# Biases of two more attention tiles on TensorE, a new opening and a new order in a fused attention and MLP kernel

## Chip, core and metric

The kernel runs on one core of a Trainium2 chip. The metric is the device time of one execution in microseconds; a profile is one profiled execution, and its span runs from the first instruction to the last.

## What is computed

```python
scores = 0.125 * q @ k^T                       # 4 batches, 8 heads, 768 positions, head size 64
keep = (key < 8) | (0 <= query - key < 96)     # 8 global keys, and the 96 last ones
bias = -slope[h] * dist                        # dist = 96 for global keys outside the window
a = softmax(where(keep, scores + bias, -1e9))
x = (a @ v) as rows of 3072 tokens x 512       # all heads of a token side by side
out = relu(x @ w_in) ** 2 @ w_out              # w_in 512 x 2048, w_out 2048 x 512
```

## The kernel before

The 3072 tokens are 24 tiles of 128 (tile j; six to a batch), and 12 blocks of two tiles for the MLP. For each tile: q, k and v are loaded and cast; q and k are transposed (`tr.n.j` on PE, n = 0 for q and 1 for k, and the copy `T.n.j` out of the bank; from tile 8 on by a DMA); `sc` multiplies them into four banks of 128 x 512 scores (head group g, odd or even head; two banks in the first tile of a batch), which hold the tile's own keys and those of the tile before; `exp.j.odd.g` on ACT takes the exponential out of one bank; `pv` multiplies with v, `norm` divides by the sum on DVE, and `trx` with `xT` transposes the result for the MLP. `gk` and `gv` copy the eight global rows of k and v to the tile.

The mask and the bias enter in one of two ways. For tiles under `NBIAS` a matmul ahead of the scores puts them into the bank: `bias.j` multiplies a scaled identity `sid[h]` with the mask `pb`, eight matmuls of 256 columns (of 128 in the first tile of a batch). For the others ACT takes the exponential of the bare scores, and `mul.j.g` on DVE multiplies it by `E`, the exponential of the mask, or by `E0` (made from E) in the first tile of a batch.

The MLP's first layer of blocks 0 and 1 is eight steps `s1.blk.s`, each of one piece of w_in (`win`), with `relu` and `sq`; `s1.0.0` to `s1.0.3` are cut in parts (#1 to #4). From block 2 on it is seven products in place of eight (`h`, with `xs`, `isum`, `u`, `c`, `q` around them); the second layer is `s2`, likewise with `sum`, `wsum`, `part`, `o` and the store `st`.

At the start DVE zeroes a buffer `zero`, and PE multiplies it with itself `NWARM` times (512 columns each). DVE makes `ident32`, `ident`, `pb` and `sid`, and ACT makes E in eight exponentials. Tile 0's q and k come through SP's queue as 32-bit numbers (`plain`); every other load is issued by POOL, which casts to bf16. A second set of `NKEEP` matmuls with `zero`, the operation `warm`, stands behind the transposes of tile 0's q.

The order is written out: a string `ORDER` has one word for each operation, with the bank numbers behind a colon and the engine behind an @; the operations are emitted in that order, so each engine's queue is the order of its words.

```python
nc.scalar.activation(junk, zero[:, :1], Act.Exp)
for i in range(NWARM):
    nc.tensor.matmul(out=banks[7], lhsT=zero[:, :P], rhs=zero, start=True, stop=True)
for g in range(2):
    for odd in range(2):
        for i in range(2):
            nc.scalar.activation(E[:, odd, g, i], pb, Act.Exp, scale=float(slopes[4 * g + 2 * i + odd]))
# per tile
if j < NBIAS:
    bias = plan.op(("bias", j, gs[0]), {"PE": 0.056 * n}, ...)
```

Lines of the profile: 310 and 307 loads, 319 the loads of `plain`, 372 the first warm matmuls, 532 the second, 506 `tr`, 429, 431 and 433 copies by ACT, POOL and DVE, 579 `bias`, 599 `sc`, 665 `exp`, 690 `mul`, 748 `pv`, 778 and 779 `norm`, 816 `trx`, 1061 `s1`, 950 `h`, 1212 and 1339 `s2`, 1287 `o`.

Of the kernel before, what the change touches and what calls it, by code (L numbers as in the profile page):

```python
# [62 lines left out]
T.1.4@V xT.1@V pv.2.1:0 ld.k.5 ld.win.2.0 exp.3.1.1 gk.3@A ld.win.2.1 norm.2.0 s1.0.3:2 mul.3.0 s1.0.6:4 ld.win.4.0
tr.0.4:7 ld.q.5 ld.v.4 norm.2.1 mul.3.1 relu.0.6@A s1.0.3#2 gv.2@P pv.3.0:3 norm.3.0 trx.2:5 T.0.4@A pv.3.1:6
ld.win.1.0 norm.3.1 ld.win.0.1 xT.2@A sc.4.0:1047 exp.4.1.1 exp.4.1.0 tr.1.5:3 T.1.5@A s1.0.2:5 trx.3:6 xT.3@V
ld.win.0.0 ld.win.5.0 s1.0.2#2 s1.0.2#3 s1.0.2#4 relu.0.3@V exp.4.0.1 ld.v.5 gv.3@P exp.4.0.0 gk.4@V sq.0.6@V
relu.0.2@A s1.1.3:7 ld.win.7.0 relu.1.3@A load.6 s1.1.6:0 mul.4.1 tr.0.5:6 mul.4.0 sq.0.3@V s1.1.2:3 T.0.5@A ld.wout.3
pv.4.0:2 ld.wout.1 sq.0.2@V sc.5.0:4157 ld.wout.0 s1.0.4:6 relu.1.2@A exp.5.1.1 s1.0.1:3 sq.1.3@A exp.5.0.0 relu.0.4@V
s1.1.4:7 ld.wout.2 norm.4.0 pv.4.1:4 gv.4@P norm.4.1 sq.0.4@A load.7 exp.5.1.0 sq.1.2@A relu.1.4@A s1.0.0:6 gate.9
ld.wout.4 mul.5.0 s1.0.0#2 sq.1.4@A s1.0.0#3 s1.1.5:2 trx.4:1 exp.5.0.1 relu.1.6@V s1.1.1:4 ld.wout.5 s1.0.1#2  # L70
relu.1.1@A E0.1 mul.5.1 relu.1.5@A pv.5.0:7 s1.1.7:0 s1.1.0:5 sq.1.1@V norm.5.0 ld.wout.6 E0.0 sq.1.5@V tr.1.6:4
sq.1.6@A pv.5.1:2 relu.1.7@A tr.0.6:7 s1.0.0#4 norm.5.1 xT.4@A sq.1.7@A h.2.0.p2:0 ld.wout.7 T.1.6@V h.2.1.p2:1
trx.5:2 xT.5@V relu.1.0@A sq.1.0@A gate.14 h.2.0.p1:5 xs.2.0 s1.0.5:4 sum.1.2 s1.0.7:2 relu.0.1@A xs.2.1 gate.10
sum.1.0 sum.1.1 relu.0.0@A T.0.6@A sc.6.0:36 wsum.0.0 sum.1.3 sq.0.0@A sq.0.1@A s2.0.0.0:7 relu.0.7@A s2.0.1.0 load.9
exp.6.0.0 xs.2.2 s2.0.2.0 exp.6.1.0 s2.0.3.0 s2.0.0.1:2 s2.0.1.1 wsum.2.0 relu.0.5@A sq.0.7@A s2.0.2.1 load.8 mul.6.0
wsum.1.0 s2.0.3.1 tr.0.7:3 tr.1.7:6 gate.15 isum.0.0 h.2.1.p1:4 T.0.7@A s2.0.4.0 isum.0.1 s2.1.p1.0:3 isum.3.1 T.1.7@A
sq.0.5@A pv.6.0:6 isum.1.1 s2.0.4.1 s2.0.5.1 u.2.0.1@A c.2.0.c11 s2.0.5.0 gate.11 u.2.1.1@A h.2.1.p6 q.2.0.c11@A
isum.1.0 T.8 s2.0.6.1 u.2.1.2@A s2.0.6.0 isum.3.0 pv.6.1:0 h.2.0.p6 wsum.2.1 wsum.0.1 s2.1.p1.1 s2.0.7.1 c.2.1.c11
norm.6.0 gate.13 o.0.1@V st.0.1 s2.0.7.0 h.2.1.p7 part.1.p1@A s2.1.p6.0 u.2.0.2@A o.0.0@A u.2.1.3@A h.2.0.p7 h.2.1.p4
T.9 norm.6.1 wsum.3.0 u.2.0.3@A sc.7.0:1762 c.2.1.c21@A wsum.1.1 h.2.1.p5:0 c.2.1.c22 q.2.1.c11@A s2.1.p2.0:4  # L80
exp.7.1.0 exp.7.0.0 isum.2.1 load.10 h.2.0.p4 exp.7.0.1 mul.7.0 exp.7.1.1 s2.1.p2.1 isum.2.0 s2.2.p1.0:7 q.2.1.c21@A
mul.7.1 h.2.0.p5:1 s2.1.p6.1 part.1.p6@A trx.6:6 gate.12 c.2.0.c21@A load.12 pv.7.0:2 xT.6@A c.2.0.c22 q.2.1.c22@A
q.2.0.c22@A s2.2.p1.1 h.2.1.p3 s2.1.p7.0 wsum.3.1 o.1.p2 norm.7.0 h.2.0.p3 pv.7.1:5 s2.1.p7.1 q.2.0.c21@A st.0.0
c.2.1.c12 s2.1.p5.0 s2.1.p5.1 part.1.p7@A q.2.1.c12@A s2.1.p4.0 T.10 s2.1.p4.1 c.2.0.c12 gk.7@V q.2.0.c12@A o.1.p5
o.1.p4@A sc.8.0:6201 st.1.1 part.2.p1@A s2.1.p3.0 norm.7.1 sum.2.0 sum.2.1 s2.1.p3.1 trx.7:5 xT.7@V o.1.p3 h.3.0.p1:3
exp.8.1.0 gk.8@V h.3.1.p1:2 exp.8.0.0 exp.8.1.1 exp.8.0.1 h.3.0.p2:6 xs.3.0 u.3.1.1@A sc.9.0:1540 s2.2.p6.0 mul.8.0
xs.3.1 mul.8.1 u.3.0.1@A h.3.0.p6 exp.9.0.1 exp.9.1.1 gv.7@V h.3.1.p2:4 c.3.0.c11 h.3.1.p6 c.3.1.c11 exp.9.0.0
pv.8.0:0 s2.2.p6.1 pv.8.1:6 load.11 norm.8.0 u.3.1.2@A s2.2.p2.0:1 sum.2.2 gv.8@P q.3.1.c11@A norm.8.1 xT.8 h.3.1.p7
h.3.0.p5:4 u.3.0.2@A h.3.0.p7 s2.2.p2.1 exp.9.1.0 st.1.0 part.2.p6@A xs.3.2 u.3.1.3@A q.3.0.c11@A h.3.1.p5:0 s2.2.p7.0
u.3.0.3@A mul.9.1 mul.9.0 s2.2.p7.1 c.3.1.c22 T.12 c.3.0.c22 pv.9.0:6 h.3.1.p3 o.2.p2 h.3.0.p4 c.3.1.c12 load.15  # L90
norm.9.0 q.3.1.c22@A h.3.0.p3 s2.3.p1.0:5 s2.3.p1.1 c.3.0.c12 q.3.0.c22@A pv.9.1:0 c.3.0.c21@A part.2.p7@A norm.9.1
q.3.1.c12@A h.3.1.p4 q.3.0.c12@A h.4.0.p1:3 c.3.1.c21@A s2.2.p5.0 part.3.p1@A gk.9@V sc.10.0:6402 s2.2.p5.1
q.3.0.c21@A sum.3.0 sum.3.1 s2.2.p4.0 s2.2.p4.1 exp.10.1.0 sum.2.3 exp.10.0.0 exp.10.0.1 h.4.0.p2:4 T.11 u.4.0.1@A
exp.10.1.1 gk.10@V gv.9@A s2.3.p6.0 o.2.p5 mul.10.0 c.4.0.c11 xT.9 h.4.1.p1:6 o.2.p4@A mul.10.1 s2.2.p3.0 s2.2.p3.1
q.3.1.c21@A s2.3.p2.0:0 sum.3.2 u.4.1.1@A pv.10.0:2 pv.10.1:4 s2.3.p6.1 xs.4.0 gate.17 o.2.p3 part.3.p6@A xs.4.1
s2.3.p2.1 norm.10.0 h.4.0.p6 h.4.1.p6 q.4.0.c11@A gv.10@A norm.10.1 u.4.0.2@A load.13 s2.3.p7.0 sc.11.0:7124 u.4.1.2@A
sum.3.3 h.4.0.p7 h.4.1.p7 xs.4.2 exp.11.1.0 o.3.p2 exp.11.0.0 u.4.0.3@V s2.3.p7.1 sc.12.0:17 exp.11.1.1 exp.11.0.1
gate.16 xT.10 h.4.0.p4 c.4.0.c21@A mul.11.0 st.2.0 mul.11.1 h.4.1.p2:4 c.4.1.c11 exp.12.1.0 s2.3.p5.0 pv.11.0:2
pv.11.1:3 s2.3.p5.1 norm.11.0 part.3.p7@A h.4.0.p5:7 q.4.1.c11@A u.4.1.3@A norm.11.1 h.4.1.p5:4 q.4.0.c21@A gate.20
s2.3.p4.0 c.4.0.c22 load.14 s2.3.p4.1 h.4.0.p3 T.13 gate.18 load.16 c.4.1.c22 exp.12.0.0 h.4.1.p4 q.4.1.c22@A h.4.1.p3  # L100
xT.11 s2.4.p2.0:2 h.5.0.p1:3 q.4.0.c22@A o.3.p5 mul.12.0 c.4.0.c12 o.3.p4@A c.4.1.c21@A u.5.0.1@A c.4.1.c12 T.15
s2.3.p3.0 q.4.0.c12@A s2.3.p3.1 q.4.1.c12@V q.4.1.c21@A h.5.0.p2:1 o.3.p3 sc.13.0:5764 st.3.1 st.2.1 h.5.1.p1:0
# [5 lines left out]
c.5.0.c12 q.5.0.c21@A kl.15@V part.4.p7@A c.5.1.c22 q.5.0.c12@A sc.14.0:1346 o.4.p5 s2.4.p4.0 xT.13 exp.14.0.1 kl.14@V
h.5.1.p3 gv.13@P q.5.1.c22@V c.5.1.c12 c.5.1.c21@A s2.4.p4.1 load.17 h.6.0.p1:4 s2.4.p3.0 s2.4.p3.1 exp.14.1.1
exp.14.1.0 exp.14.0.0 sc.15.0:0673 mul.14.1 mul.14.0 xs.6.0 o.4.p4@A xs.6.1 h.6.0.p2:1 o.4.p3 q.5.1.c12@A s2.5.p1.0:5  # L110
u.6.0.1@A c.6.0.c11 exp.15.0.0 exp.15.1.0 exp.15.1.1 sum.5.0 s2.5.p1.1 h.6.0.p6 u.6.0.2@A exp.15.0.1 sum.5.1 load.18
h.6.0.p5:2 part.5.p1@A pv.14.0:0 norm.14.0 pv.14.1:6 h.6.1.p1:1 u.6.1.1@A h.6.0.p7 gv.14@P st.4.0 s2.5.p6.0 u.6.0.3@A
# [96 lines left out]

# [1222 lines left out]
```

## Time and profile before

| | us |
|---|---|
| three runs | 198.62, 199.34, 199.52 |
| median | 199.34 |
| span of the profiled execution | 197.6 |
| PE busy | 191.9 |
| DVE busy | 173.2 |
| ACT busy | 163.0 |
| POOL busy | 80.4 |

The page gives no time of the profiled execution beside its span; the runs were timed apart from it. Busy is the time in which at least one of an engine's instructions ran. Matmuls are pipelined: where many stand in a row, their length by a row of the chain over their number is the pace, while the length of one alone (0.22 us for 128 columns) has the way through the array in it. In a row of the timeline the first number is the start from the span's begin, the second the length, and the brackets tell how long the engine stood idle before and who ended that.

### The profile page before, as it was taken

How to read it: one execution, taken by the hardware profiler on the slowest of the kernel's cores; microseconds unless marked ns; L12 is line 12 of the kernel's file. 1: busy time of each engine (PE TensorE's matmuls, PEld its weight loads, DVE VectorE, ACT ScalarE, POOL GpSimd, SP SyncE). 2: the span in 40 equal slices, each digit the busy share in tenths (PEclk: the TensorE clock that was granted, in tenths of full speed). 3: DMA queues.
4: the chain of work that ended last, by engine and by line, in shares of the span. 5: the costliest groups of instructions: out<-in, count | busy, mean ns of one | idle time of the engine just before them, and what ended most of it. 6: DMA issues, size and time to landing. Idle time of an engine off the chain costs nothing.

```text
span 197.6 us, 6777 instructions
## 1 busy us (share of the span) xinstructions
PE 191.9 (97%) x2776; PEld 169.6 (86%) x2776; DVE 173.2 (88%) x423; ACT 163.0 (82%) x335; POOL 80.4 (41%) x101
## 2 busy tenths in 40 slices
PE   7989999999999999999999999999999999999993
PEld 3578999866989999899989999989899989999992
DVE  8159869999999999799999999999899999989872
ACT  6379989966999898999789998998989879774750
POOL 8999988586045309603192903080410001000000
PEclk9999999999999999999999999999999999999999
DMA  6999999999999999999999999999695711114023
GB/s 127 153 158 171 181 181 185 182 202 159 139 209 191 75 200 88 145 174 210 151 129 203 114 124 194 160 121 92 136 81 116 154 55 56 27 30 163 0 106 106
DMA packets 111857, 26.91 MB, mean 136 GB/s; under 512 B 103379, under 2 KB 109011, under 8 KB 111827
## 3 DMA queue, kind: packets, MB, share of 16 engines
q0 software_dynamic: 80256, 13.37, 91.8%
q1 hardware_dynamic: 31570, 13.11, 32.5%
q8 instruction: 21, 0.34, 0.6%
q14 instruction: 10, 0.07, 0.1%
HBM read 27.26 MB, written 6.29 MB: 170 GB/s over the span
## 4 chain that ended last, share of the span: by engine, by line
PE 95%; DVE 2%; issue 1%; ACT 0%; DVEq 0%
PE bank L1212 35%; PE bank L950 32%; PE bank L1061 7%; PE bank L599 6%; PE bank L748 5%; PE bank L1339 4%; PE bank L372 2%; PE bank L506 2%; PE bank L532 1%; DVE qkT L433 1%; PE bank L816 1%; PE bank L579 0%; ACT qkT L429 0%; DVE o L1287 0%; DVE v L433 0%
## 5 line engine op out<-in xcount | busy, mean ns | idle before, releaser
L1015 ACT ACTIVATE hs<-hr 128x512 bf16<-128x512 f32 x72 | 44.8, 641 | 5.1 <-DVE hr L995 4.7
L665 ACT ACTIVATE esc<-bank 128x512 bf16<-128x512 f32 x78 | 42.9, 614 | 1.3 <-PE bank L599 1.0
L1212 PE MATMUL bank<-wsum,hsum 128*128 128x256 bf16 x264 | 36.2, 273 | 0.0
L1212 PEld LDWEIGHTS <-hsum 128*128 128x128 bf16 x360 | 32.1, 98 | 4.1 <-issue 0.5
L995 DVE CUSTOM_DVE_ANT_0 hr<-bank,early 128x512 f32<-128x512 f32 x45 | 30.4, 685 | 2.5 <-PE bank L950 1.5
L950 PEld LDWEIGHTS <-win 128*128 128x128 bf16 x480 | 29.7, 98 | 1.0
L950 PEld LDWEIGHTS <-qk_first 128*128 128x128 bf16 x480 | 29.7, 98 | 1.0
L429 ACT COPY early<-bank 128x512 f32<-128x512 f32 x42 | 24.5, 591 | 3.6 <-PE bank L950 3.3
L690 DVE TENSOR_TENSOR at<-esc,E 128x1024 bf16<-128x1024 bf16 x39 | 26.7, 696 | 0.1
L1212 PEld LDWEIGHTS <-hs 128*128 128x128 bf16 x264 | 24.0, 98 | 2.6
L310 POOL DMA_DIRECT2D qk<-in_q_dram x18 | 16.0, 890 | 21.9 <-DMA qkT<-qk 20.6
L1212 PE MATMUL bank<-wout,hs 128*128 128x256 bf16 x176 | 24.9, 273 | 0.0
L310 POOL DMA_DIRECT2D v<-in_v_dram x18 | 16.0, 888 | 18.3 <-DVE v L480 14.9
L950 PE MATMUL bank<-xT,win 128*128 128x128 bf16 x320 | 23.4, 219 | 0.0
L431 POOL COPY v<-v 8x520 bf16<-8x520 bf16 x8 | 5.7, 718 | 43.3 <-PE bank L748 43.3
L950 PE MATMUL bank<-xs,qk_first 128*128 128x128 bf16 x320 | 22.8, 219 | 0.0
L779 DVE TENSOR_TENSOR x<-bank,rs 128x256 bf16<-128x256 f32 x48 | 20.4, 425 | 1.7
L865 ACT ACTIVATE hr<-bank 128x512 f32<-128x512 f32 x33 | 19.4, 598 | 1.3 <-PE bank L950 0.4
L748 PE MATMUL bank<-v,at 128*128 128x65 bf16 x352 | 17.8, 193 | 0.0
L1287 DVE TENSOR_TENSOR o<-bank,part 128x256 f32<-128x256 f32 (+2 forms) x34 | 13.8, 410 | 3.3 <-PE bank L1212 3.2
L429 ACT COPY part<-bank 128x256 f32<-128x256 f32 x29 | 10.9, 375 | 7.1 <-PE bank L1212 6.9
L310 POOL DMA_DIRECT2D qk<-in_k_dram x18 | 16.1, 897 | 0.9 <-DMA win<-in_moe_w_in_dram 0.5
(92 smaller groups left out, 367.0 us busy)
## 6 DMA issues: line engine op xcount, KB each, us to landing
out_dram<-o SPq DMA_DIRECT2D x22, 256.0 KB, 2.5
v<-in_v_dram POOLq DMA_DIRECT2D x24, 128.0 KB, 5.6
qk<-in_q_dram POOLq DMA_DIRECT2D x18, 128.0 KB, 5.0
qk<-in_k_dram POOLq DMA_DIRECT2D x18, 128.0 KB, 5.8
wout<-in_moe_w_out_dram POOLq DMA_DIRECT2D x8, 256.0 KB, 8.5
win<-in_moe_w_in_dram POOLq DMA_DIRECT2D x6, 256.0 KB, 6.9
qk_first<-in_k_dram POOLq DMA_DIRECT2D x5, 128.0 KB, 5.6
qk_first<-in_q_dram POOLq DMA_DIRECT2D x5, 128.0 KB, 5.7
```

Source lines behind the costliest of these rows:

```text
L310: nc.gpsimd.dma_start(out=dst, in_=src)
L429: nc.scalar.copy(dst, src)
L665: nc.scalar.activation(out=tiles[tag, j, g][:, odd], in_=tiles.pop(("sc", j, odd, g)).rearrange("p a c -> p (a c)"), func=Act.Exp, scale=s ...
L690: nc.vector.tensor_mul(at, tiles.pop(("esc", j, g)), bias)
L748: nc.tensor.matmul(out=po[:, hi, :], lhsT=tiles["at", j, g][:, odd, at * P : (at + 1) * P], rhs=v_sb[kj][:, h, :], start=(i == 0), stop=(i ...
L779: nc.vector.tensor_tensor(out=x[:, 4 * hf : 4 * hf + 4, :], in0=po[:, :, :D], in1=rs.to_broadcast([P, 4, D]), op=Alu.mult,)
L865: nc.scalar.activation(dst, src, Act.Relu)
L950: nc.tensor.matmul(out=tiles["h", blk, g, bank][:, n], lhsT=left_[:, s, k], rhs=right_[:, k], start=opens and n == 0 and k == 0, stop=k == ...
L995: nc.vector._custom_dve(TENSOR_ADD_SAT, out=hr, in0=src, in1=tiles.pop(("u", blk, g, i)), s0=float("inf"), s1=0.0,)
L1015: nc.scalar.activation(hs, hr, Act.Square)
L1061: nc.tensor.matmul(out=hT[:, c, cols], lhsT=w_in_sb[s][:, kt, c * P : (c + 1) * P], rhs=tiles["xT", blk][:, kt, cols], start=(kt == 0), st ...
L1212: nc.tensor.matmul(out=tiles["acc", blk, bank][:, cols], lhsT=left_[:, s], rhs=right_[:, cols], start=first and s == 0, stop=s == NSTEP - ...
```

## The change

1. `NBIAS` goes from 3 to 5: the bias and mask of tiles 3 and 4 are put into the banks by PE, and their four multiplications on DVE go.
2. `zero` and its memset go; the first warm matmuls use a constant of ones that is written ahead of the program, 16 of 224 columns in place of 8 of 512.
3. The operation `warm` (8 matmuls of 512 columns) goes.
4. The eight exponentials of E become operations `E.odd.g.i` of the order; the multiplications and E0 depend on them.
5. The order is new throughout, the order of the loads and the choice of engines with it: k and q of tile 1 are loaded first, and the piece `win.3.0`, which was first, is ninth.

```diff
-    NBIAS = 3
+    NBIAS = 5
-    zero = early[:, 1, 2 * P :].bitcast(BF16)
-    NWARM = 8
-    NKEEP = 8
+    NWARM, NWCOL = 16, 224
-    nc.vector.memset(zero.bitcast(I32), 0)
+    one = nc.const_aps.tensor(1.0, [P, NWCOL], BF16)
-    nc.scalar.activation(junk, zero[:, :1], Act.Exp)
+    nc.scalar.activation(junk, one[:, :1], Act.Exp)
     for i in range(NWARM):
-        nc.tensor.matmul(out=banks[7], lhsT=zero[:, :P], rhs=zero, start=True, stop=True)
+        nc.tensor.matmul(out=banks[7][:, :NWCOL], lhsT=one[:, :P], rhs=one, start=True, stop=True)
+    maskE = {}
-                nc.scalar.activation(
-                    E[:, odd, g, i], pb, Act.Exp, scale=float(slopes[4 * g + 2 * i + odd])
+                def emit_E(e, g=g, odd=odd, i=i):
+                    nc.scalar.activation(
+                        E[:, odd, g, i], pb, Act.Exp, scale=float(slopes[4 * g + 2 * i + odd])
+                    )
+                maskE[odd, g, i] = plan.op(
+                    ("E", odd, g, i), {"ACT": 0.32}, emit_E, key=-1.0, ready=4.0,
                 )
-            ready=8.0,
+            deps=[m for (o, _, _), m in maskE.items() if o == odd],
-        if j == 0:
-            def emit_warm(e):
-                for _ in range(NKEEP):
-                    nc.tensor.matmul(out=psum(), lhsT=zero[:, :P], rhs=zero, start=True, stop=True)
-            plan.op(("warm",), {"PE": 0.216 * NKEEP}, emit_warm, key=base)
-                deps=exps + (maskE0 if first else []),
+                deps=exps + (maskE0 if first else [m for (_, gg, _), m in maskE.items() if gg == g]),
 ORDER
-tr.0.0:0 warm:7 tr.1.0:1 T.1.0@V bias.0.0:23 T.0.0@A sc.0.0 ld.win.3.0 exp.0.0.0 ld.k.1 tr.1.1:4 bias.1.0:5670 T.1.1@V ld.q.1
+ld.k.1 ld.q.1 E.0.0.1 ld.q.2 E.0.1.0 E.1.1.0 tr.0.0:0 ld.v.0 E.1.0.0 ones.6 T.0.0@A ld.k.2 tr.1.0:1 ld.q.3 bias.0.0:23
```

What it moves is shown at four places. The first is POOL's queue at the start (`qk_first` holds q and k of tiles 1 to 5, `v_0` and `v_1` v of tiles 0 and 1), before:

```order
L367 IOTA early_103 128x256
L307 DMA win_93<-in_moe_w_in_dram 128x4x256
L307 DMA qk_first_66<-in_k_dram 128x8x64
L307 DMA qk_first_66<-in_q_dram 128x8x64
L307 DMA v_0_71<-in_v_dram 128x8x64
L307 DMA qk_first_66<-in_q_dram 128x8x64
L307 DMA qk_first_66<-in_k_dram 128x8x64 x2
```

and after:

```order
L360 IOTA early_103 128x256
L300 DMA qk_first_66<-in_k_dram 128x8x64
L300 DMA qk_first_66<-in_q_dram 128x8x64 x2
L300 DMA v_0_71<-in_v_dram 128x8x64
L300 DMA qk_first_66<-in_k_dram 128x8x64
L300 DMA qk_first_66<-in_q_dram 128x8x64
L300 DMA v_1_72<-in_v_dram 128x8x64
L300 DMA qk_first_66<-in_k_dram 128x8x64
L300 DMA win_93<-in_moe_w_in_dram 128x4x256
```

The piece of w_in went from the first place to the ninth, and tile 1's k and q lead.

The second is PE around the transposes of tile 0's q (bank 0, `bank_107`) and k (bank 1, `bank_108`), before, with the last rows of the second warm set:

```order
L532 LDWEIGHTS early
L532 MATMUL bank_114<-early 128x512
L506 MATMUL bank_108<-ident_100,plain 128x128 x4
L579 LDWEIGHTS early
L579 MATMUL bank_109<-pb_105,early 128x128
```

and after:

```order
L365 LDWEIGHTS const-bfloat16-1.0
L365 MATMUL bank_114<-const-bfloat16-1.0 128x224
L505 MATMUL bank_107<-ident_100,plain 128x128 x4
L505 MATMUL bank_108<-ident_100,plain 128x128 x4
L572 LDWEIGHTS early
L572 MATMUL bank_109<-pb_105,early 128x128
```

Nothing stands between the two transposes any more.

The third is ACT's queue from the masks to the exponentials of tile 2 (the casts and copies into `qkT` are T, the small one of 128x4x8 is gk; the exponentials write `at`), before:

```order
L397 ACTIVATE E_101<-pb_104 128x256 x8
L429 CAST qkT_0_81<-bank_0_107 128x512
L665 ACTIVATE at_198<-bank_2_109 128x512
L665 ACTIVATE at_198<-bank_3_110 128x512
L665 ACTIVATE at_238<-bank_7_114 128x512
L665 ACTIVATE at_238<-bank_0_107 128x512
L665 ACTIVATE at_277<-bank_6_113 128x512
L429 COPY qkT_1_82<-qkT_0_81 128x4x8
L429 COPY qkT_2_83<-bank_1_108 128x512
```

and after:

```order
L392 ACTIVATE E_101<-pb_104 128x256 x4
L428 CAST qkT_0_81<-bank_0_107 128x512
L428 CAST qkT_0_81<-bank_1_108 128x512
L658 ACTIVATE at_212<-bank_3_110 128x512
L392 ACTIVATE E_101<-pb_104 128x256 x2
L658 ACTIVATE at_212<-bank_2_109 128x512
L658 ACTIVATE at_244<-bank_6_113 128x512
L428 COPY qkT_1_82<-qkT_0_81 128x4x8
L428 COPY qkT_2_83<-bank_5_112 128x512
L658 ACTIVATE at_244<-bank_7_114 128x512
```

Four masks stay ahead, two went between the exponentials of tile 0, and k of tile 0 is now cast by ACT (before by DVE).

The fourth is the order's last words. Before, the second piece of the last product, `s2.11.p3.1#2`, came behind the sum `o.11.p3` of the first piece: `s2.11.p3.0 s2.11.p3.1 s2.11.p3.0#2 o.11.p3 s2.11.p3.1#2 st.11.0#2 o.11.p3#2 st.11.0#3`. Now it comes ahead of it: `s2.11.p3.0 o.11.p4 s2.11.p3.1 st.11.1#2 s2.11.p3.0#2 s2.11.p3.1#2 o.11.p3 st.11.0#2 o.11.p3#2 st.11.0#3`.

More of the change, by code (lines that the diff above doesn't have):

```diff
@@ L63 @@
[L63 to L102, printed above, removed]
@@ L108 @@
[L108 to L112, printed above, removed]
@@ L158 @@
[L158 to L160 removed]
+ld.k.1 ld.q.1 E.0.0.1 ld.q.2 E.0.1.0 E.1.1.0 tr.0.0:0 ld.v.0 E.1.0.0 ones.6 T.0.0@A ld.k.2 tr.1.0:1 ld.q.3 bias.0.0:23
+T.1.0@A tr.1.1:4 ld.v.1 sc.0.0 T.1.1 tr.0.1:5 exp.0.1.0 bias.1.0:6701 T.0.1 ld.k.3 E.0.0.0 E.0.1.1 sc.1.0 exp.0.0.0
@@ new lines @@
+ld.win.6.0 pv.3.1:5 norm.3.0 sc.4.0 ld.win.4.0 norm.3.1 s1.0.0:0 exp.4.1.0 s1.0.0#2 gv.3@P trx.2:6 exp.4.0.1 trx.3:4
+xT.2 s1.0.0#3 sq.0.3 s1.0.0#4 ld.win.2.0 xT.3 tr.0.5:5 tr.1.5:2 T.0.5 s1.1.3:7 load.6 T.1.5@A gk.4 relu.0.0 s1.1.0:6
+relu.1.3@V exp.4.0.0 exp.4.1.1 sq.0.0@V sc.5.0:4520 s1.0.5:3 exp.5.1.0 ld.win.2.1 exp.5.1.1 pv.4.0:7 exp.5.0.1 ld.v.5
+s1.0.1:1 norm.4.0 relu.0.5 s1.1.1:5 gate.11 ld.win.7.0 exp.5.0.0 pv.4.1:0 E.1.1.1 mul.5.0 s1.1.6:2 sq.1.3 gv.4@P
+norm.4.1 sq.0.5 s1.0.4:7 load.7 mul.5.1 relu.1.6 s1.0.1#2 sq.1.6@V s1.1.5:3 relu.1.0@V relu.0.4@V trx.4:4 s1.1.4:0
@@ new lines @@
+load.12 h.2.0.p3 c.2.0.c21 s2.0.7.1 wsum.0.1 s2.0.7.0 o.0.1 pv.7.0:3 wsum.2.0 s2.1.p1.1 q.2.1.c22 wsum.1.1 h.2.1.p4
+part.1.p1 pv.7.1:7 norm.7.0 c.2.1.c21 s2.1.p6.0 wsum.2.1 s2.1.p6.1 o.0.0 h.2.1.p3 norm.7.1 part.1.p6 q.2.0.c21
+sc.8.0:5320 st.0.1 c.2.0.c12 h.3.0.p1:7 exp.8.1.0 gv.7 q.2.1.c21@V trx.7:4 exp.8.0.0 s2.1.p7.0 T.10 gk.8 exp.8.0.1
+c.2.1.c12 h.3.0.p2:3 exp.8.1.1 s2.1.p2.0:5 xT.7 s2.1.p2.1 mul.8.0 q.2.1.c12 s2.1.p7.1 u.3.0.1 o.1.p2 sc.9.0:2140 mul.8.1
+q.2.0.c12 s2.1.p5.0 c.3.0.c11 exp.9.0.1 load.11 s2.1.p5.1 exp.9.1.1 gate.13 sum.2.0 pv.8.1:4 part.1.p7 pv.8.0:3 xs.3.0
```

143 lines of the change are left out of this document (86 added, 57 removed).

## The prediction

> **What bounds the kernel now.** I read the page's busy shares and chain first, then stretches of the span, then the opening instruction by instruction, then the landings of the loads, then the end.
>
> ```profile
> PE 191.9 (97%) x2776; PEld 169.6 (86%) x2776; DVE 173.2 (88%) x423; ACT 163.0 (82%) x335; POOL 80.4 (41%) x101
> PE 95%; DVE 2%; issue 1%; ACT 0%; DVEq 0%
> 0.00:17.90 17.90, 15.36 (x173) 10.38 (x174) 9.98 (x45) 11.28 (x26) 17.10 (x25) 1.00 1.79 150
> 17.90:193.90 176.00, 176.00 (x2604) 158.97 (x2601) 162.59 (x378) 151.68 (x311) 63.33 (x77) 1.00 1.21 135
> 10.00 0.87 PE bank L579 x8
> 18.29 1.32 PE bank L1061 x16
> 20.52 0.22 PE bank L816 x4
> 21.11 0.55 PE bank L599 x16
> 161.76 2.18 PE bank L1212 x20
> ```
>
> The first line is the page's busy time, the second its chain by engine, the next two are stretches (PE first, then weight loads, DVE, ACT, POOL), the rest are pieces of the chain (start, us, what). PE is the chain for 95% of the span. From 17.9 us to 193.9 us it is busy in all 176.00 us, and twenty 256-column matmuls in 2.18 us are 0.109 us each, the same 0.109 as the eight of a bias in 0.87 us: matmuls follow each other at one rate, and nothing is waited for. So in that stretch every added column on PE costs its time, and work taken off DVE or ACT brings nothing unless PE waits for it. Time can be gained in the opening 17.9 us and behind 193.9 us only.
>
> ```profile
> 0.74 0.45 SPq L319 DMA_DIRECT2D plain<-in_q_dram  x1
> 0.86 0.27 DVE L361 MEMSET early<- 128x256 int32 x1 [0.86 <-PEq L1413]
> 1.19 3.60 PE L372 MATMUL bank<-early 128*128 128x512 bf16 x8 [1.19 <-DVE early L361]
> 1.25 0.56 SPq L319 DMA_DIRECT2D plain<-in_k_dram  x1
> 1.34 0.89 POOL L307 DMA_DIRECT2D win<-in_moe_w_in_dram  x1 [0.17 <-issue]
> 2.22 0.90 POOL L307 DMA_DIRECT2D qk_first<-in_k_dram  x1
> 3.20 2.56 ACT L397 ACTIVATE E<-pb 128x256 bf16<-128x256 bf16 x8 [0.96 <-DVE pb L386]
> 4.58 1.06 PE L506 MATMUL bank<-ident,plain 128*128 128x128 f32 x4
> 5.43 2.62 PE L532 MATMUL bank<-early 128*128 128x512 bf16 x8
> 7.89 0.60 PE L506 MATMUL bank<-ident,plain 128*128 128x128 f32 x4
> 8.53 0.69 DVE L433 CAST qkT<-bank 128x512 bf16<-128x512 f32 x1 [3.55 <-PE bank L506]
> 9.71 1.09 ACT L665 ACTIVATE at<-bank 128x512 bf16<-128x512 f32 x2 [3.44 <-PE bank L599]
> 12.26 1.57 ACT L665 ACTIVATE at<-bank 128x512 bf16<-128x512 f32 x3 [1.46 <-PE bank L599]
> 13.70 0.23 ACT L429 COPY qkT<-qkT 128x32 bf16<-128x32 bf16 x1
> 13.81 0.61 ACT L429 COPY qkT<-bank 128x512 bf16<-128x512 bf16 x1
> 16.65 0.23 PE L599 MATMUL bank<-qkT 64*128 64x128 bf16 x2 [0.29 <-DVE qkT L433]
> 21.45 0.22 PE L599 MATMUL bank<-qkT,qkT 64*128 64x128 bf16 x2
> plain<-in_q_dram SPq DMA_DIRECT2D x1, 256.0 KB, 3.1
> plain<-in_k_dram SPq DMA_DIRECT2D x1, 256.0 KB, 6.0
> win<-in_moe_w_in_dram POOLq DMA_DIRECT2D x1, 256.0 KB, 5.7
> qk_first<-in_k_dram POOLq DMA_DIRECT2D x1, 128.0 KB, 5.7
> ```
>
> These are rows of the timeline (start, length, engine, line, in brackets the idle time before) and, last, of the DMA view (us from issue to landing, for the first issue of each). PE spends 1.19 to 4.58 on the first warm matmuls and 5.43 to about 7.7 on the second set, both without use for the result. What follows hangs on one instruction: the transposes of tile 0's k at 7.89. They could not have begun before 1.25 + 6.0 = 7.25, when that k landed. Behind them the cast (8.53), the first scores, and the first exponential at 9.71; the scores of tile 3 begin at 16.65, those of tile 4 end at 21.67. I call the start of k's transposes D: D is 7.89, the scores of tile 4 end at D + 13.8.
>
> **The change, part by part.**
>
> *Biases of tiles 3 and 4 on PE.* Sixteen 256-column matmuls at 0.109 us: +1.74. The four multiplications that go from DVE release nothing, since PE waits for DVE nowhere in 17.9 to 193.9. In the new order the bias of tile 3 stands before T.1.3, which ACT gives late (next point), so most of it fills a wait; the bias of tile 4 stands in dense work.
>
> *ACT's order.* Before, all eight mask exponentials (2.56 us, 0.32 each) lay in 3.20 to 5.76, where ACT had nothing else. Now four stand there, two (0.64 us) between the two exponentials of tile 0, one ahead of tile 4's, one later. ACT is serial here. Counted on from D with the rows' pitches (0.52 for one of three exponentials in 1.57, 0.59 for a copy, 0.11 from the small copy to the next): the first exponential starts at D + 1.75 (9.71 less 7.89, and the cast is an ACT copy of some 0.6 in place of 0.69); then one exponential, two masks, two exponentials, the small copy, T.1.2, seven exponentials and T.1.3 are ten times 0.53, 0.64, 0.11 and two times 0.55: 7.2 us, with two hand-overs of 0.1 about D + 9.1. The scores of tile 3 can then begin; before they began at 16.65 = D + 8.76. So they are some 0.4 later behind D, with tile 3's bias done. From there to the end of tile 4's scores stand on PE 0.55 (scores), 0.22, 0.46, 0.89, 0.45, 0.87 (bias of tile 4), 0.46 and 0.55 us, and two waits for DVE (the copy of v's global rows stands behind a relu there) of some 0.3 and 0.1: 4.9, so about D + 14.1 against D + 13.8. But at that point the new order has not done two pieces that the old one had: s1.0.6 (eight 256-column matmuls, 0.87) and trx.2 (0.22). Behind D the new opening is therefore 0.3 + 1.1, about 1.4 to 1.6 us the longer: I take 1.6, as small hand-overs are left out. Were both biases hidden it would be 0; were neither, and the two masks on the chain too, 1.74 + 0.64 = 2.4. The value lies nearest to the walk through the rows.
>
> *Warm matmuls and zeros.* The second set (2.4 us before D) goes; the first set is 16 times 224 columns, at 427 ns per 512 columns (3.60 us for eight, less the fill) 0.19 each, 3.0 us, from a constant that POOL writes ahead of the program, so about 0.4 sooner than behind the memset: it ends near 3.8, beside the landing of q at 0.74 + 3.1 = 3.84. The memset that goes (0.27 us on DVE) was beside other work: 0.
>
> *Loads of tile 1 first.* The 256 KB of w_in that POOL issued first move behind eight others, so each of these lands one issue pitch earlier (0.88, from 1.34 to 2.22): tile 1's k at some 6.4 instead of 7.95. More weight lies on tile 0's k, which goes through SP's queue: 6.0 us against q's 3.1, and it landed at 7.25 just behind w_in's 1.34 + 5.7 = 7.04. I read this as sharing with that transfer. With half the size beside it I put it 0.85 earlier, at 6.4, so D is 6.45. Bounds: no gain, 7.3; as fast as q, 4.4, where PE itself is busy until 4.8: D in 4.8 to 7.3, the gain 0.6 to 3.1. I take 7.89 − 6.45 = 1.44. Seven pitches and its own larger size behind that k, the w_in piece lands at about 13.5, ahead of its first use at some 17; v and the later tiles land as early as before or earlier. SP's queue has the same issues up to there.
>
> ```profile
> PE bank L1212 <- DVE o L1287: 0.5, 1, 0.5
> 193.18 0.94 PE L1212 MATMUL bank<-wout,hsum 128*128 128x192 bf16 x12
> 194.16 0.36 DVE L1287 TENSOR_TENSOR o<-bank,part 128x192 f32<-128x192 f32 x1 [0.84 <-PE bank L1212]
> 194.57 0.28 PE L1212 MATMUL bank<-wout,hsum 128*128 128x64 bf16 x4 [0.45 <-DVE o L1287]
> 194.88 0.22 DVE L1287 TENSOR_TENSOR o<-bank,part 128x64 f32<-128x64 f32 x1 [0.37 <-PE bank L1212]
> ```
>
> *The end* (a row of the waits, four of the timeline). PE's last four matmuls wait 0.5 us for the sum of the first 192 columns. The new order puts them ahead of that sum. They then end 0.5 sooner, but the sum starts 0.1 later and the second follows it directly: the last one ends near 194.85 instead of 195.10, and the two stores still go one behind the other through SP: −0.1, between 0 and −0.3.
>
> *The rest of the order.* About equal numbers of instructions on ACT and DVE, and PE without a wait before. I take 0; the bounds are −0.2 and +0.8, since an order with a new wait can only lose where nothing was lost.
>
> *Sum.* −1.44 + 1.6 − 0.1 = +0.06. The profiled span is 197.6; the median run is 199.34, 1.74 above it, which I take as the time around the span. So 197.66 and 199.4. The three runs spread over 0.9 us, so the profiled one may be up to half a microsecond from the median.
>
> **Rivals.**
>
> *The clock rises later (slower).* Until about 6.8 us PE ran at half speed: the first set took 427 ns per 512 columns (216 by the rate of the long stretch), of the second, eight in 2.62 us, some three did, and k's transposes took 0.60 where q's took 1.06. Before, PE was busy without a gap from 1.19 to 7.7. Now it stands idle from the end of q's transposes (about 4.8) to D. If that delays the rise to some 10 us, the work between D and there (0.60, 0.45, 0.22, 0.40, 0.22 and the bias of tile 1, 0.87: 2.8 us) runs at half speed, and as ACT hides some of it, about 1.3 us is lost, between 0.7 and 2.0: 200.7. It decides from the point at which the clock is still half when D comes. For it: the rise came 5.6 us into gapless work before. Against: the new first set begins earlier and is followed by q's transposes, 3.9 us in one piece.
>
> [...]
>
> *Tile 0's k is not earlier.* If 6.0 us is SP's own time, D is 7.3: the gain is 0.6, and the time 200.2. For it: the transfer was issued as the second of its queue.
>
> *The opening gains all round (faster).* With w_in out of the way k lands by 5.3, D is 5.4, and tile 3's and 4's biases lie in waits (cost 0.8 in place of 1.6): −2.5 + 0.8 − 0.1 = −1.8, or 197.6; half of it is 198.5. Against: ACT's chain holds it then, and v of tile 0 and k of tile 2, which by the pitch land three and four issues behind tile 1's k, near 9 and 9.8.
>
> **How the numbers follow.** The forecast case 0.42 (199.4, own range 198.6 to 200.3), the late clock 0.32 (200.0 to 201.4), k not earlier 0.08, the faster opening 0.18. A difference under 0.5% (1.0 us) cannot be told from none here. Faster than 198.3: two thirds of the last case and little of the first, 0.16. Slower than 200.3: most of the late clock and half of the third case, 0.32. Same: 0.52. The range 198.0 to 201.2 leaves out the ends of the second and the last case.
>
> **What would show it.** The profile after should have k's transposes near 6.5 at 0.60 us; tile 3's scores near 15.6 behind an ACT copy, with PE idle before them; tile 4's scores ending near 20.6; no stretch with idle PE behind 21; 0.5 us less wait at the end. Wrong would be: transposes of 1.06 us at D (the clock), a D of 7.3 or 5.4 (the load), or waits on PE past 21 us (the order).

## The result and the profile after

| | runs | median us | ratio to the kernel before |
|---|---|---|---|
| before, same chip | 198.62 to 199.52 | 199.29 | |
| after | 200.25, 201.02, 201.22, 203.34, 203.43 | 201.22 | 1.0084 (1.0056 to 1.0113) |

The new kernel is 0.8% slower; 1.0084 times the 199.34 us shown before is 201.0. Here and below, a run more than 1.5% above the fastest of its kernel (here the two over 203 us) is left out of the ratio, though not of the median. Its profiled execution was the fastest of the five, 200.25 us with a span of 198.5. The page's busy times and chain, two stretches (PE, weight loads, DVE, ACT, POOL), and the one row that PE's waits between 20 and 194 us have:

```profile
PE 191.9 (97%) x2792; PEld 171.0 (86%) x2792; DVE 175.6 (88%) x424; ACT 159.6 (80%) x328; POOL 80.8 (41%) x102
PE 35%; POOL 1%; DVE 0%; DVEq 0%; issue 0%
0.00:17.90 17.90, 15.88 (x215) 12.67 (x216) 11.52 (x49) 13.96 (x31) 17.08 (x25) 1.00 1.84 151
17.90:193.90 176.00, 175.06 (x2566) 157.53 (x2564) 163.59 (x374) 145.28 (x298) 63.72 (x78) 1.00 1.24 135
PE bank L592 <- DMA qkT<-qk: 0.5, 1, 0.5
```

The stretch in which PE had been busy for all 176.00 us now has 0.94 us of idle PE, 0.65 of it behind 21 us, and a name stands beside PE's longest wait that the old trace did not have: a DMA transpose. The chain's shares sum to little more than a third, so its followed part is of less use here than the stretches. The opening and the end, as rows of the timeline, and the landing of tile 0's k from the DMA view:

```profile
plain<-in_k_dram SPq DMA_DIRECT2D x1, 256.0 KB, 4.0
0.78 3.15 PE L365 MATMUL bank<-const-bfloat16-1.0 128*128 128x224 bf16 x16 [0.78 <-PEq L1406]
4.28 1.66 PE L505 MATMUL bank<-ident,plain 128*128 128x128 f32 x8 [0.35 <-DMA plain<-in_q_dram]
14.60 0.23 PE L592 MATMUL bank<-qkT 64*128 64x128 bf16 x2 [0.48 <-ACT qkT L428]
19.52 0.22 PE L592 MATMUL bank<-qkT,qkT 64*128 64x128 bf16 x2
193.80 1.06 PE L1205 MATMUL bank<-wout,hsum 128*128 128x192 bf16 x16
194.90 0.49 DVE L1280 TENSOR_TENSOR o<-bank,part 128x192 f32<-128x192 f32 x2 [1.22 <-PE bank L1205]
194.40 0.95 SPq L1302 DMA_DIRECT2D out_dram<-o  x1
```

The eight transposes of q and k are one row; the second four begin at 5.27, just behind k's landing (issued 1.26, 4.0 later). So D is 5.27, 2.62 earlier than before, and tile 4's scores end at 19.74.

To place the difference I add to 20 us the matmuls that PE has still to do, each at its pace in the dense stretch. That is when PE would end if it waited for nothing more. It separates opening, middle and end (us, all from one profile each; for a few traces with two or three missing matmul records the work is taken from the complete ones):

| profile | end by the work left at 20 us | PE's last matmul | lost in between | from there to the span's end |
|---|---|---|---|---|
| before | 188.80 | 194.65 | 5.85 | 2.95 |
| after | 188.31 | 194.66 | 6.35 | 3.82 |

Most of the 5 to 6 us lost in between is the change between the score matmuls on 64 rows and all others on 128: from 20 us on the old kernel has some twenty changes each way, of about 0.12 us from 64 rows to 128 and 0.10 back, beyond the pace. PE counts as busy in them, and every version has them. The old end has 0.62 of it in the wait before its last four matmuls, which in the new order lies behind PE's last matmul. So the opening, with both biases paid, is 0.49 ahead; the middle loses 6.35 − (5.85 − 0.62) = 1.12; the end loses 3.82 − (2.95 + 0.62) = 0.25. The sum is +0.88, which is the difference of the spans. The middle is the largest term, and larger still in other executions.

### The profile page after: what moved, and what is told of

Same layout as the page of the kernel before. It is cut to its first block, busy times and chain, and to the rows that moved or that the text cites. A ratio compares the mean times of both kernels' runs of the same rounds, so it can differ in the third digit from the quotient of the medians.

```text
span 198.5 us, 6809 instructions
## 1 busy us (share of the span) xinstructions
PE 191.9 (97%) x2792; PEld 171.0 (86%) x2792; DVE 175.6 (88%) x424; ACT 159.6 (80%) x328; POOL 80.8 (41%) x102
## 2 busy tenths in 40 slices
DMA packets 111857, 26.92 MB, mean 136 GB/s; under 512 B 103378, under 2 KB 109010, under 8 KB 111826
## 5 line engine op out<-in xcount | busy, mean ns | idle before, releaser
L1008 ACT ACTIVATE hs<-hr 128x512 bf16<-128x512 f32 x67 | 41.1, 634 | 5.0 <-DVE hr L988 4.8
L658 ACT ACTIVATE esc<-bank 128x512 bf16<-128x512 f32 x70 | 38.5, 602 | 2.1 <-PE bank L592 1.7
L1205 PE MATMUL bank<-wsum,hsum 128*128 128x256 bf16 x264 | 35.4, 273 | 0.1
L428 ACT COPY early<-bank 128x512 f32<-128x512 f32 x41 | 23.7, 591 | 5.6 <-PE bank L943 4.8
L683 DVE TENSOR_TENSOR at<-esc,E 128x1024 bf16<-128x1024 bf16 x35 | 23.8, 682 | 0.8 <-ACT esc L658 0.5
L943 PE MATMUL bank<-xT,win 128*128 128x128 bf16 x320 | 24.3, 219 | 0.0
L1205 PE MATMUL bank<-wout,hs 128*128 128x256 bf16 x176 | 24.1, 273 | 0.0
L943 PE MATMUL bank<-xs,qk_first 128*128 128x128 bf16 x320 | 23.6, 219 | 0.0
L858 ACT ACTIVATE hr<-bank 128x512 f32<-128x512 f32 x31 | 18.7, 608 | 3.2 <-PE bank L943 2.0
L741 PE MATMUL bank<-v,at 128*128 128x65 bf16 x352 | 17.9, 193 | 0.3 <-DVE v L432 0.3
L741 PEld LDWEIGHTS <-at 128*128 128x128 bf16 x352 | 15.6, 98 | 1.7 <-issue 0.5
```

What stands on the lines that cost most here:

```text
L428: nc.scalar.copy(dst, src)
L658: nc.scalar.activation(out=tiles[tag, j, g][:, odd], in_=tiles.pop(("sc", j, odd, g)).rearrange("p a c -> p (a c)"), func=Act.Exp, scale=s ...
L683: nc.vector.tensor_mul(at, tiles.pop(("esc", j, g)), bias)
L741: nc.tensor.matmul(out=po[:, hi, :], lhsT=tiles["at", j, g][:, odd, at * P : (at + 1) * P], rhs=v_sb[kj][:, h, :], start=(i == 0), stop=(i ...
L858: nc.scalar.activation(dst, src, Act.Relu)
L943: nc.tensor.matmul(out=tiles["h", blk, g, bank][:, n], lhsT=left_[:, s, k], rhs=right_[:, k], start=opens and n == 0 and k == 0, stop=k == ...
```

## The experiments

First four asked which part of the change costs the time: the clock and the idle PE of the opening, the middle's order, the end, or the biases. Runs are given as medians beside the old kernel's median on the same chip.

### The new kernel once more

No edit.

> The changed kernel once more, unaltered, to see what differs between executions. Its first profile (span 198.5) had tile 0's k transposes at 5.3 us and the full clock from 5.0 us, three waits that the old order does not have (sum about 1.1 us past 20 us, the longest 0.5 us for a DMA transpose of tile 11 at 76.9) and an end 0.9 us longer behind PE's last matmul. Theory A (clock): executions differ by when PE's clock rises; a longer one shows transposes of k at 1.06 instead of 0.60 us and the scores of tile 3 at about 16 instead of 14.6. Theory B (loads): the opening is the same, and longer executions wait longer for DMA transposes between 60 and 130 us. Both: median 200.3 to 201.3, that is 1.005 to 1.010 of the kernel before.

201.34 beside 199.57, ratio 1.0091 (1.0050 to 1.0133). Its stretch, and PE's wait rows between 20 and 194 us:

```profile
17.90:193.90 176.00, 174.04 (x2553) 156.67 (x2554) 162.63 (x372) 145.41 (x298) 63.83 (x78) 1.00 1.25 134
PE bank L1205 <- DVE o L1280: 0.7, 1, 0.7
PE bank L592 <- DMA qkT<-qk: 0.7, 2, 0.5
103.67 0.42 DVE L1280 TENSOR_TENSOR o<-bank,part 128x256 f32<-128x256 f32 x1 [0.67 <-DMA out_dram<-o]
```

The opening was the same (188.3 by the work left at 20 us), the clock rose early (4.05 us into the span), and PE's last matmul came 1.17 later than in the first profile. The wait for DVE is one for a transfer too: the last row shows DVE's sum `o` held 0.67 us until an earlier store had left its buffer. The loss is in the middle and differs from execution to execution.

### PE kept busy in the opening

```diff
-    NWARM, NWCOL = 16, 224
+    NWARM, NWCOL, NKEEP = 19, 224, 4
+            plan.op(("warm",), {"PE": 0.1 * NKEEP}, emit_warm, key=base)
 ORDER
- tr.0.0:0
+ tr.0.0:0 warm:7
```

> The changed kernel with PE kept busy until tile 0's k has landed: 19 instead of 16 warm matmuls, and 4 more of them between the transposes of tile 0's q and of k. Theory A (clock): the late rise goes, and the runs come together near the shortest ones of the changed kernel, 200.2 to 200.7. Theory B (loads): the spread stays, and the median is the changed kernel's, or up to 0.4 later as k's transposes begin at about 5.7 instead of 5.3.

203.07 beside 199.57, ratio 1.0176 (1.0138 to 1.0215). The opening stood 0.4 ahead of the new kernel's, and the middle lost 4 us more:

```profile
30.85 0.40 PE L505 MATMUL bank<-ident,qk 128*128 128x128 bf16 x4 [0.20 <-DMA qk<-in_q_dram]
31.52 0.40 PE L505 MATMUL bank<-ident,qk 128*128 128x128 bf16 x4 [0.27 <-DMA qk<-in_k_dram]
55.69 0.23 PE L598 MATMUL bank<-qkT 64*128 64x128 bf16 x2 [0.75 <-DMA qkT<-qk]
```

PE reached tile 6's transposes and tile 8's scores before their transfers had landed. The clock rose at 4.67 us here, early, and the kernel was slower still: a late clock is not the cause.

### The new kernel with the old end

```diff
-s2.11.p3.0#2 s2.11.p3.1#2 o.11.p3 st.11.0#2
+s2.11.p3.0#2 o.11.p3 s2.11.p3.1#2 st.11.0#2
```

> The changed kernel with one word moved back: the last four matmuls (second piece of s2.11.p3.1) behind the sum of the first 192 columns, as before. If the end's 0.9 us come from that word: the sum of 192 columns begins 0.24 us behind the last matmul of the first piece again, the time from it to the last landing is as before, and the kernel is 0.3 to 0.9 us shorter. Rival: the 0.9 us come from SP, whose store ahead of them took 0.95 us to issue in place of 0.40, which the word does not touch: then at most 0.3, and the long issue comes and goes by itself.

201.79 beside 199.57, ratio 1.0115 (1.0085 to 1.0146). From the start of the last sixteen matmuls to the span's end it took 4.5 us (195.40 to 199.9), against 4.7 and 4.4 (193.80 to 198.5, 194.97 to 199.4) in the two profiles of the new end and 4.4 (193.18 to 197.6) before. As far as four profiles tell, the two ends are worth the same; what moves them is how long SP takes to issue one store (`st.11.1#2`), 0.95 in the row above, 0.70 to 0.73 in three others and 0.40 in the old kernel. Why it differs is not shown.

### The old kernel with two more biases

`NBIAS` 5; `bias.3.0` and `bias.4.0` ahead of their scores, the four multiplications out.

> The kernel before with one part of the change: biases of tiles 3 and 4 by PE, each right ahead of its scores, and their four multiplications on DVE left out; all else in the old order. Theory 1 (PE has no idle time past 17.9 us, so each column counts): 16 matmuls of 0.109 us, +1.7 us, less what of tile 3's lies in the wait ahead of its scores (0.45 us): +1.3 to +1.7. Rival (DVE and ACT are the hidden limit in 20 to 50 us, and 2.8 us less on DVE pay for the columns): 0 or shorter.

200.84 beside 199.57, ratio 1.0059 (1.0037 to 1.0080): 1.2 us, of 1.74 on PE. PE waited for nothing between 20 and 194 us. The biases alone cost two thirds of what the whole change costs, and yet they do not explain it: the new opening has already paid for them and is ahead.

### The old order with two parts of the new opening

```diff
-    NKEEP = 8
+    NKEEP = 0
 ORDER
- sc.0.0 ld.win.3.0 exp.0.0.0
+ sc.0.0 exp.0.0.0
- T.1.3@V ld.k.4 pv.1.0:4
+ T.1.3@V ld.k.4 ld.win.3.0 pv.1.0:4
```

> The old order with two things of the new opening alone: the piece win.3.0 goes from the first place of POOL's queue to the ninth, and the second warm set is left out (NKEEP 0); three biased tiles, the zeros and the mask exponentials as before. Theory B (the new order's loss lies behind 20 us, in scores and products set too close behind what they read; the opening itself gains): tile 0's k lands near 5.2, its transposes start near 5.7 instead of 7.89, of the 2.2 us 1.5 to 2.2 are kept, and behind 20 us nothing waits: 197.4 to 198.1, ratio 0.989 to 0.993. Rival R (the middle is held by its loads, whatever the order, and an earlier opening only runs into them): the start is as early, but waits appear between 40 and 100 us and the time is 198.8 to 199.6. Rival C (the second warm set kept the clock): the clock rises behind 8 us, k's transposes take 1.06, 199 to 200.

199.60 beside 199.08, ratio 1.0015 (0.9989 to 1.0040): no gain. Tile 0's k landed at 5.17, D was 5.41, and at 20 us the kernel stood 0.8 ahead of the old one (188.0). Its last matmul came at 194.96, 0.31 behind the old one's. Two rows show where the lead went; the third is the second one's place before:

```profile
33.90 0.40 PE L504 MATMUL bank<-ident,qk 128*128 128x128 bf16 x4 [0.40 <-DMA qk<-in_k_dram]
105.28 0.43 DVE L920 TENSOR_TENSOR xs<-xT 128x512 bf16<-128x512 bf16 x1 [0.82 <-DMA xT<-x]
104.77 0.42 DVE L922 TENSOR_TENSOR xs<-xT 128x512 bf16<-128x512 bf16 x1
```

An earlier PE meets loads and DMA transposes that are not earlier. Before, `xT` took 4.9 us from issue and landed at 104.67, and DVE took it up at 104.77 without a wait, but with 0.1 us to spare; here it was issued 0.4 earlier, took 5.8 and landed at 105.26. For that `xs` PE then waited 0.54 us. The old order's 176.00 busy us had hidden this: it had no wait and, at such places, no reserve.

### The old kernel without its second warm set

`NKEEP` 0, loads as before.

> The old kernel without its second warm set (NKEEP 0), loads unchanged. If the 256 KB of w_in beside tile 0's k set its landing, k lands near 7.25 as before, its transposes start near 7.3, and the time is 0.3 to 0.6 less, 198.8 to 199.1, the clock having risen by then or not. If PE itself (the warm set) was what the start waited for, k lands well before 7 us and the gain is over 1 us, under 198.4. Rival C: PE idle from 5.6 to 7.3 keeps the clock at half until 10 us: 200 to 200.8.

199.51 beside 199.08, ratio 1.0019 (0.9993 to 1.0045).

```profile
4.40 1.35 PE L506 MATMUL bank<-ident,plain 128*128 128x128 f32 x8
8.08 0.40 PE L506 MATMUL bank<-ident,qk_first 128*128 128x128 bf16 x4 [1.14 <-DMA qk_first<-in_k_dram]
106.78 0.34 PE L950 MATMUL bank<-xs,qk_first 128*128 128x128 bf16 x3 [0.86 <-DVE xs L922]
```

k landed at 5.05 with w_in's piece beside it, against 7.25 in the old kernel, 7.74 with five biases and 6.79 in a later run of the same opening (the old order with loads left out, below), and 5.17 to 5.7 in the profiles in which w_in came ninth. So with that piece beside it k landed later in three profiles and as early in one: that the piece held it up is not shown. D was 5.10, and 1.14 us of it went to tile 1's k, at 8.08. Of the 2.8 us that D gained, 0.8 were left at 20 us and none at the end: the early k did not bring the time under 198.4 that was to follow from it.

### The new opening before the old rest

The new kernel's first 116 words, then the old order's words.

> The new kernel with its own first 116 words (up to the copy xT.3, near 22 us) and from there the words of the old order, without the four multiplications of tiles 3 and 4. Theory B: the opening of the new kernel stands about 0.5 us ahead of the old one with both biases paid, and the old rest has no waits: 198.6 to 199.2, ratio 0.995 to 0.999. Rival 'biases': the 1.74 us of the biases are the loss, as in the old order with five biased tiles: 200.3 to 200.8. Rival R (an earlier opening runs into the loads): 199.3 to 200.3 with waits for loads or DMA transposes between 40 and 100 us.

209.19 beside 199.08, ratio 1.0515 (1.0486 to 1.0545). A miss of the experiment itself: the old rest wants another piece of w_in next than the new opening had ordered.

```profile
25.32 1.89 PE L1058 MATMUL bank<-xT,win 128*128 128x256 bf16 x8 [4.71 <-DMA win<-in_moe_w_in_dram]
20.40:25.30 4.90, 0.22 (x4) 0.04 (x1) 0.62 (x2) 0.12 (x1) 4.79 (x6) 1.00 1.62 187
25.30:32.10 6.80, 5.55 (x36) 4.43 (x37) 1.39 (x2) 2.66 (x5) 3.70 (x5) 0.50 1.99 173
```

It cannot tell what the old middle would be worth. It shows that an order of work and an order of loads belong together, and what came behind a long wait of PE: after the 4.71 us the granted clock (the last number but two) is 0.50 for 6.8 us.

### More reserve in the new order

`sc.8.0` behind `s2.1.p7.0`, `sc.9.0` behind `s2.1.p5.1`; `load.11` and `load.12`, `T.11` and `T.12` exchanged.

> The new kernel with its three tight places loosened: the scores of tile 8 stand behind three more pieces of PE's work and those of tile 9 behind two, and the load and DMA transpose of tile 11 go ahead of those of tile 12. Theory B: the waits of 0.4 to 0.6 us of PE for a DMA transpose at 54 and at 77 us go, 0.7 to 1.1 us in all: 200.2 to 200.6 against the new kernel's 201.3, ratio 1.003 to 1.006. Rival: the waits move to another input (the banks, the exponentials behind the later scores) and the time stays at 201.0 to 201.5; or the loss lies in waits elsewhere that differ from run to run, and the time stays as well.

203.17 beside 199.08, ratio 1.0203 (1.0160 to 1.0246): worse by 2 us. The waits for DMA transposes at the three places did go; the reserve (from the transpose's landing to its scores) became 1.3, 2.2 and 4.8 us, from 0.24, 0.48 and 0.05. In their place came:

```profile
56.37 0.33 PE L943 MATMUL bank<-xT,win 128*128 128x128 bf16 x3 [0.47 <-ACT esc L658]
60.68 0.31 PE L741 MATMUL bank<-v,at 128*128 128x65 bf16 x5 [0.68 <-ACT esc L658]
87.69 0.38 PE L1205 MATMUL bank<-wsum,hsum 128*128 128x256 bf16 x2 [1.43 <-ACT part L428]
86.50 0.87 ACT L428 COPY kl<-qkT 128x512 bf16<-128x512 bf16 x2 [1.38 <-DMA qkT<-qk]
```

The later scores make the exponentials late (the first two rows), and the exchange, which sets `load.15` behind `T.12`, made tile 15's DMA transpose late, landing at 86.47 instead of 83.19; for it ACT's copy `kl` stood, and behind it `part`, and PE (the last two).

### Old and new with most loads left out

By now two theories were left for the middle: transfers (R), or hand-overs between PE, ACT and DVE (H). The next three leave out the loads of later tiles. Their output is therefore not the one asked for, and they serve for their time alone.

```diff
             def emit_load(e, j=j):
-                load_v(j)
-                load_part(0, j)
-                load_part(1, j)
+                if j < 10:
+                    load_v(j)
+                if j < 9:
+                    load_part(0, j)
+                    load_part(1, j)
```

> The old kernel without the loads of q and k of tiles 9 to 23 and of v of tiles 10 to 23 (the buffers keep what an earlier tile left there, all computation and all DMA transposes stay). It is the base for the two that follow. Theory R (the DMA engines, busy nine tenths to 155 us, set landing times that no order moves; the old order meets them without a wait): PE waited for no transfer, so 198.6 to 199.4, as the old kernel. If it becomes over 1 us faster, the old order was held by transfers too, and the trace of before hid it.

> The new kernel with the same loads left out (q and k of tiles 9 to 23, v of tiles 10 to 23). Theory R: the waits for DMA transposes at 54 and 77 us and the wait near 104 us go, 1.0 to 2.2 us, and the time is 199.2 to 200.3, ratio 1.000 to 1.006; the landing of tile 8's DMA transpose comes 4 us behind its issue instead of 7.7. Rival H (hand-overs between PE, ACT and DVE in the new order): with the transfers gone PE waits for ACT and DVE in the same places, 200.8 to 201.5.

> The old order with w_in's first piece ninth and without the second warm set, with the same loads left out. Theory R: of the 0.8 us that its opening stands ahead at 20 us, 0.4 are lost at 33 us to the load of tile 6, which stays, and the loss near 105 us to the DMA transpose xT is gone: 198.2 to 198.9, ratio 0.994 to 0.998. Rival H: the lead is lost to ACT and DVE all the same, 199.3 to 199.8.

| | median us | ratio to the kernel before (199.52) |
|---|---|---|
| old order, loads left out | 199.31 | 0.9987 (0.9965 to 1.0009) |
| new order, loads left out | 199.50 | 1.0010 (0.9986 to 1.0034) |
| old order with the early opening, loads left out | 198.85 | 0.9975 (0.9952 to 0.9998) |

This decides for R in the main. Without those loads the old order gains nothing that can be measured, and the new one stands at 1.0010 instead of 1.0084 and 1.0091, where H would have left it at 200.8 to 201.5. Beside its own base, the old order with the same loads left out, it is still some 0.2% slower (0.44 us between the means of the twelve runs, with an uncertainty of 0.35): about three quarters of the loss go with the loads, and what the rest is was not tested. The new order from 40 to 110 us with and without them, and one transfer each, tile 8's DMA transpose (from issue to landing) in the old kernel, the new one, and the new one without the loads, with the matmul of its scores in the new one and in the one without:

```profile
40.00:110.00 70.00, 69.41 (x1019) 60.79 (x1019) 67.47 (x155) 59.92 (x126) 33.15 (x39) 1.00 1.67 164
40.00:110.00 70.00, 69.98 (x1022) 61.16 (x1021) 68.15 (x158) 60.55 (x128) 4.06 (x5) 1.00 0.62 105
qkT<-qk SPq DMA_TRANSPOSE x1, 3.7
qkT<-qk SPq DMA_TRANSPOSE x1, 7.7
qkT<-qk SPq DMA_TRANSPOSE x1, 4.6
53.88 0.23 PE L592 MATMUL bank<-qkT 64*128 64x128 bf16 x2
54.65 0.23 PE L594 MATMUL bank<-qkT 64*128 64x128 bf16 x2
```

Put together for the three tight tiles (us; the reserve is from the transpose's landing to its scores):

| tile | before: landed, scores, reserve | after: landed, scores, reserve | after without loads: reserve |
|---|---|---|---|
| 8 | 55.22, 59.03, 3.8 | 53.64, 53.88, 0.24 | 3.9 |
| 9 | 57.26, 62.12, 4.9 | 56.93, 57.41, 0.48 | 6.6 |
| 11 | 74.39, 80.38, 6.0 | 76.81, 76.85, 0.05 | 3.1 |

The new order takes these scores 3.5 to 5.2 us earlier, while two of the three transposes land at most 1.6 earlier and the third 2.4 later. From 17.9 us on the new order's trace without the loads has PE busy for 175.98 of 176.00 us, and from 20 us it loses 5.51, against 6.35 to 7.57 with them. By the same sum the old order without the loads loses 6.11, which is 5.49 without the 0.62 of its end: the two middles are then equal. Leaving out the loads also takes their issuing off POOL (33.15 to 4.06 us busy in the first two rows). But SP issued the transposes of tiles 8 and 11 at nearly the same time with and without the loads, and it is the time to landing that fell, from 7.7 to 4.6 and from 7.6 to 3.9 us. The first two rows are with the loads, the last two without:

```profile
45.91 1.33 SPq L530 DMA_TRANSPOSE qkT<-qk  x1
69.19 2.46 SPq L530 DMA_TRANSPOSE qkT<-qk  x1
46.15 1.33 SPq L532 DMA_TRANSPOSE qkT<-qk  x1
70.05 1.30 SPq L532 DMA_TRANSPOSE qkT<-qk  x1
```

The third kernel's profiled execution was the slowest of its twelve (200.53, with a wait of 2.17 us for a v), so its trace does not stand for its median. The median is 198.85 beside 199.31, but the means of the twelve runs differ by 0.15 us with an uncertainty of 0.47: that the early opening pays once the loads are away is not shown.

### The old order, early, with two moves

`tr.0.6` exchanged with `tr.1.6`; `xT.13` ahead of `T.16`.

> The old order with w_in's first piece ninth and without the second warm set, all loads in, and two moves: tile 6's q, which lands first, is transposed ahead of its k, and the DMA transpose xT of tile 13 is issued ahead of the one of tile 16's q and k. Theory R: the waits of 0.4 to 0.6 us at 33 us and of 0.5 to 0.9 us at 105 us shrink to a third, 198.5 to 199.0, ratio 0.995 to 0.999. Rival: the lead is lost at the next landing (tile 6's k itself, the DMA transpose of tile 13 or 16): 199.3 to 199.8.

199.52 beside 199.52, ratio 1.0012 (0.9986 to 1.0038), twelve runs from 198.36 to 201.00. Its profiled execution was the fastest, 198.36 with a span of 196.6, and in it both waits were gone and the last matmul came at 193.62. The median execution keeps none of that. Which landing it then meets, its profile does not show. No version beat the old kernel with all its work done.

## Why the prediction was right or wrong

It named 199.4 and a range to 201.2; the median is 201.22, or 201.0 by the ratio, the upper end. That it lies no higher is partly luck: in the profile the opening came out 0.65 better than forecast (−0.49 at 20 us against −1.44 + 1.6) and paid for more than half of the middle's 1.12. The terms, against the first profile:

| term | predicted | measured |
|---|---|---|
| D | 7.89 to 6.45: −1.44 | 7.89 to 5.27: −2.62 |
| behind D | +1.6 | about +2.1 (−0.49 at 20 us less −2.62) |
| end | −0.1 (0 to −0.3) | +0.25 |
| rest of the order | 0 (−0.2 to +0.8) | +1.12, and more in other executions |

*D* was mis-sized, and its reason was only half right. k's 6.0 us was read as sharing with w_in's piece; with the same piece beside it k landed at 5.05 once. And D in the old kernel was not k's landing but the end of the second warm set: k had landed at 7.25, and the set's last matmul began at 7.67 and took its 0.22 to 7.89. Tile 1's k landed at 6.17 (said: 6.4), but not for the reason given: one issue pitch earlier than 7.95 is 7.07, and the rest is that it landed 4.8 us behind its issue instead of 5.7.

*Behind D* the walk through ACT's queue held: tile 3's scores began at D + 9.33 (said: 9.1) behind an ACT copy, tile 4's ended at D + 14.47 (14.1).

*The rest of the order* is the step that failed. "Matmuls follow each other at one rate, and nothing is waited for" was true of the trace, and the conclusion, that time could be gained only in the opening and at the end and that the order in between could be taken at 0, was not. A row of the page was passed over: the share of busy DMA, in 40 slices; here it stands for the old kernel, the new one, and the new one with the loads left out, and under it the old kernel's packets.

```profile
DMA  6999999999999999999999999999695711114023
DMA  8999999999999999989999999999970212212032
DMA  8999999999610599271262462211970212211132
DMA packets 111857, 26.91 MB, mean 136 GB/s; under 512 B 103379, under 2 KB 109011, under 8 KB 111827
```

To about 140 us the DMA engines were as busy as PE, with packets of which 92% are under 512 B. The old kernel's row is as full as the new one's, so a full row did not by itself make PE wait; the loss came where the new order set scores 0.05 to 0.48 us behind a landing (the table above). The bound of +0.8 was reasoned for one new wait; the first profile has one of 0.47, the second three (0.47, 0.28 and 0.75), and they differ from execution to execution.

*The rivals.* The late clock (0.32) gave the right time, 200.0 to 201.4, for the wrong reason: in the profiles of the new kernel the clock rose at 5.02 and 4.05. It does exist: without the loads it rose at 9.00 in the profiled execution, k's transposes took 1.11 us (0.67 in the new kernel's profile) and tile 3's scores began at 15.73 instead of 14.60.

```profile
5.46 1.11 PE L507 MATMUL bank<-ident,plain 128*128 128x128 f32 x4 [0.35 <-DMA plain<-in_k_dram]
15.73 0.23 PE L594 MATMUL bank<-qkT 64*128 64x128 bf16 x2 [0.36 <-ACT qkT L428]
```

That execution took 200.11 against a median of 199.50, and the work left at 20 us ended 0.67 later than in the new kernel's profile (188.98 and 188.31), of which up to 0.19 is its later D (5.46). So a late rise was worth some 0.5 in this pair and not the 1.3 of the rival. How often it strikes was not measured. k not earlier (0.08) was refuted. The faster opening (0.18) came true as an opening, with a D of 5.27, but for the biases, which were not hidden. Of its gain the middle left nothing.

*What would show it.* k's transposes at 6.5 (they came at 5.27), tile 3's scores behind an ACT copy (yes, 14.60), no idle PE behind 21 us (wrong: 0.65 us), 0.5 less wait at the end (yes, but given back behind it). "Waits on PE past 21 us (the order)" was the sign named for being wrong, and it is what came.

## What to carry to other kernels

An engine that is busy all the time in a trace does not show what stands just behind it: for each input of the dense stretch compare the landing with the use, and treat a reserve of 0.1 us as a wait that has not happened yet (at `xT`, 0.1 us of reserve became a wait of 0.54). Where the DMA row was full, an earlier start or an earlier place in the order bought nothing here (ratios 1.0015, 1.0019 and 1.0084): `xT`, issued 0.4 us earlier, landed 0.6 later, and tile 11's transpose, wanted 3.5 earlier, landed 2.4 later. Waits that were pushed away came back elsewhere (203.17 us). To tell transfers from hand-overs between engines, leave the transfers out of old and new alike, and compare these two with each other: that pair showed what the other edits had only narrowed down.
